# Attention and spectral mixing on one core: last rows of two batches by narrow products, fill products in PE's last waits, last tiles sent by two engines

## The chip, the cores and the metric

The kernel runs on one core of one Trainium2 chip. A time is the device time of one execution in microseconds (us). Comparisons are between medians of several runs. TensorE is called PE, VectorE DVE, ScalarE ACT, GpSimd POOL and SyncE SP, as in the profile.

## The reference

First a sliding-window attention with 8 batches, 8 heads, 576 positions and head size 64, window 64. Its output is x, 8 x 576 x 512. Then a spectral mix along the sequence: the 64 lowest Fourier modes of x are multiplied by one complex 512 x 512 matrix for each mode, and transformed back. Last a projection with a ReLU.

```python
scores = np.where((rel >= 0) & (rel < 64), q @ k.T / np.sqrt(D), -1e9)
x = softmax(scores) @ v                       # to (B, S, 512)
X = np.fft.rfft(x, axis=1)[:, :64]
Y = einsum('bmd,mde->bme', X, w_r + 1j * w_i) # 64 matrices for each of w_r, w_i
y = np.fft.irfft(Y, n=S, axis=1)
u = x + y
out = u + np.maximum(u @ w_ch, 0.0)           # float32, 8 x 576 x 512
```

The two stacks of 64 matrices are 134 MB in float32.

## The kernel before, in words

The order of the work is written out by hand, engine by engine; tile pools add the waits. POOL's DMA queue brings the weights and casts them to bf16 on the way, two modes (or, near the end, one) in a transfer, into two rings of buffers and into space that is lent.

*Attention* runs first, beside the first weight loads. It leaves x in `x_sb` and `x4` and its forward transform in `XQ`.

*The spectral half.* Modes go in 16 groups of four. `steps` lists the groups by halves of the channels (`hb`), and each step has a part with w_r and a part with w_i (`ri`). `mode_half` (line 162) makes one such part: 8 products (line 171) whose weights are 32 columns of `XQ` and whose moving operand is a weight tile; the four modes of a group fill four row blocks of one PSUM bank `psm`. Groups 12 and 13 (`LAST` and `LAST + 1`) come last. In the very last part the order is by mode, and the last two modes have a transfer each, so that PE can start on each as it lands. `finish_group` (line 595) casts a finished group to bf16 (`stg`); the inner function `prepare` puts it in order by products with `sel`: transposed into `pt` (line 612), and for groups 12 and 13 also as rows into `py` (line 619).

Between the parts PE has other products to do, which `advance` deals out: `transposed` and `multiply` give XW = x @ w_ch for each of the 36 output tiles (`x_jobs`), and `batch_job` gives for each batch the rows Y (`yrows`) and Z = Y @ w_ch (`zrows`). Y and Z have 128 rows of modes for each batch. Batch 0 has tiles of its own, `Y0` and `Z0`; the others lie in `Yall` and `Zall`. The 16 rows that come from groups 12 and 13 are not there yet at that point and are put in later.

*The inverse transform and the output.* 36 tiles of 128 positions: for each batch four, and after each pair of batches one with the last 64 positions of both. A tile i needs

- u = x + trigI^T Y: `tail_x` (an identity product that puts x into PSUM bank `pu[i]`), `tail_u` (products with `trigI`, then a copy to SBUF by ACT; for odd tiles below 33 there is no identity product, and DVE adds x instead: `by_dve`);
- p = XW + trigIr^T Z: `tail_xw` (an identity product) and the product with `trigIr` in `tail_out`;
- out = u + relu(p): in `tail_out`, by DVE at line 756, or, for the tiles of `by_dve`, by ACT and POOL at line 754. SP sends the tile to memory (line 760); a tile with the last positions of two batches goes in two halves.

`tail_u` runs four tiles ahead (`AHEAD`).

*Around the change.* After the last wi product PE makes `tail_xw(0)` and `tail_xw(1)`, and then the two groups' last rows are finished for all batches together: `prepare` for group 13 (here called `select`), a copy of `pt` to `tr` by ACT, a copy of `py` to `yst` by DVE, four products `pz` = tr^T w_ch (line 774), a copy to `zst` (line 780). Two DMAs by SP spread `yst` and `zst` over the rows of `Yall` and `Zall` (lines 770 and 781). Batch 0, with which the output begins, does not wait for them: products with every eighth column of an identity (lines 777 and 785) pick its 16 rows out of `yst` and `zst`, and copies put them into `Y0` and `Z0` (lines 778 and 786).

```python
        y0 = bank("y")
        nc.tensor.matmul(out=y0[0:16], lhsT=ident_bf[:, 0:128:B], rhs=yst, start=True, stop=True)
        z0 = bank("p")
        nc.tensor.matmul(out=z0[0:16], lhsT=ident_r[:, 0:128:B], rhs=zst, start=True, stop=True)
```

Of the kernel before, what the change touches and what calls it, by code (L numbers as in the profile page):

```python
# [11 lines left out]
BF16 = mybir.dt.bfloat16  # L12
# [14 lines left out]
def kernel(  # L27
# [41 lines left out]
    sel = consts.tile([128, 4, 16], BF16, name="sel")  # L69
    trigF = consts.tile([128, NTF, 2 * NM], BF16, name="trigF")  # L70
# [93 lines left out]
    def mode_half(psm, grp, hb, ri, first, last):  # L164
        pairs = range(4 * grp, 4 * grp + 4)
        order = [(j, p) for j in range(NJ) for p in pairs]
        if (grp, hb, ri) == (*steps[-1], 1):
            order.sort(key=lambda jp: (jp[1], jp[0]))
        for j, p in order:
            g = p % 4  # L170
            nc.tensor.matmul(out=psm[32 * g:32 * g + 32, :],  # L171
# [6 lines left out]
        spent.update(i for i, (_, ps, *of) in enumerate(wlist) if ps[0] in pairs and of == [hb, ri])  # L178

    with tc.manual_schedule():  # L180
# [321 lines left out]
        stgpool = pool("stgpool", bufs=4, reuse_waits="tile")  # L502
        Y0 = zpool.tile([128, DM], BF16, name="Y0")
        Z0 = zpool.tile([128, DM], FP32R, name="Z0")
        rowpool = pool("rowpool", reuse_waits="tile")
# [57 lines left out]
        def yrows(b):  # L563
            return Yall[:, b, :] if b else Y0

        def zrows(b):
            return Zall[:, b, :] if b else Z0
# [27 lines left out]
        def finish_group(grp, psm):  # L595
# [12 lines left out]
            rows = slice(16 * (grp // 2), 16 * (grp // 2) + 16)  # L608

            def prepare():  # L610
# [3 lines left out]
                if not end:  # L614
                    if i:
                        k0 = 8 * (grp - 1)
                        nc.scalar.copy(out=YT[:, :, :, k0:k0 + 16], in_=pt.rearrange("p c (k b) -> p b c k", b=B))
                    return
                nc.tensor.matmul(out=py[64 * i:64 * i + 64, :], lhsT=lanes, rhs=stg, start=True, stop=True,
                                 tile_position=(0, 64 * i))  # L620
            if grp == LAST + 1:
                late["last"] = prepare, rows
            else:
                ready.append(prepare)
# [32 lines left out]

        stmp2 = pool("stmp2", side="right", reuse_waits="tile")
        tables = list(inverse_tables())
        NX0 = 10  # L660
        x_jobs(pool("xp0", reuse_waits="tile"), 0, NX0)
        psm = None
        half = given = 0
        n0, n1 = 2 * EARLY, 4 * (NGRP - EARLY)
        for i, (grp, hb) in enumerate(steps[EARLY:]):
            f, l = grp < EARLY or hb == 0, hb == 1
            if i == EARLY:
                while tables:
                    tables.pop(0)()
                while jobs or pend:  # L670
                    advance()
                close(stmp2, yp, ringB)
                Zall = pool("zall", side="right").tile([2 * NM, B, DM], FP32R, name="Zall")
                x_jobs(pool("xp1", side="right", reuse_waits="tile"), NX0, NT)
                given = 0
            if f:
                psm = bank("m")
            for ri in range(2):
                if half == n0 + n1 - 2:
                    while jobs or pend:  # L680
                        advance()
                mode_half(psm, grp, hb, ri, f, l)
                load_weights(len(wlist))
                while ready:
                    ready.pop(0)()
                for t in tables[0:2]:
                    t()
                del tables[0:2]
                if half == 0:
# [100 lines left out]
        for i in range(NT):  # L790
            tail_out(i)
            if i > 1:
                tail_xw(i + 2)
# [35 lines left out]
```

## Time and profile before

| | |
|---|---|
| median of 3 runs | 442.08 us (441.78 to 442.22) |
| profiled execution | 441.96 us |
| its span | 440.2 us |
| PE busy | 330.7 us (75%) |
| DVE busy | 219.8 us (50%) |
| ACT busy | 172.8 us (39%) |
| POOL busy | 143.3 us (33%) |
| mean granted PE clock | 0.897 |

The span is from the first to the last instruction of the core; some 1.8 us of the execution lie outside it. Times in rows of the trace count from the start of the span. Matmuls overlap, and their ends are modelled, so a busy PE is not PE at its peak. In rows of the timeline stand start, duration, engine (PEld is the loading of PE's weights), line, operation, out<-in, shapes, count, and in brackets the idle time ahead with what ended it. In rows of groups, busy time and the mean ns of one follow the first bar, idle time ahead the second. In windows, PEclk is the granted clock as a share of full speed, and the DMA share is the mean of 16 DMA engines.

### The profile page before, as it was taken

How to read it: one execution, taken by the hardware profiler on the slowest of the kernel's cores; microseconds unless marked ns; L12 is line 12 of the kernel's file. 1: busy time of each engine (PE TensorE's matmuls, PEld its weight loads, DVE VectorE, ACT ScalarE, POOL GpSimd, SP SyncE). 2: the span in 40 equal slices, each digit the busy share in tenths (PEclk: the TensorE clock that was granted, in tenths of full speed). 3: DMA queues.
4: the chain of work that ended last, by engine and by line, in shares of the span. 5: the costliest groups of instructions: out<-in, count | busy, mean ns of one | idle time of the engine just before them, and what ended most of it. 6: DMA issues, size and time to landing. Idle time of an engine off the chain costs nothing.

```text
span 440.2 us, 10911 instructions
## 1 busy us (share of the span) xinstructions
PE 330.7 (75%) x4670; PEld 211.8 (48%) x4712; DVE 219.8 (50%) x445; ACT 172.8 (39%) x304; POOL 143.3 (33%) x211
## 2 busy tenths in 40 slices
PE   6888989898999997974335564675766676669994
PEld 3666767676667675651113222333443443334552
DVE  8488777876776774865004111212223122335773
ACT  6566757565666664532001110111221122113662
POOL 9333333323333223222232322122322223200773
PEclk8699999999999998997559666789899889997999
DMA  8999999999999999999999999999999999982787
GB/s 206 211 211 211 212 211 210 211 211 211 211 212 211 211 211 212 210 211 211 214 255 211 211 211 211 211 211 211 211 211 211 211 211 211 212 167 60 268 296 274
DMA packets 47873, 93.45 MB, mean 212 GB/s; under 512 B 3536, under 2 KB 3664, under 8 KB 47824
## 3 DMA queue, kind: packets, MB, share of 16 engines
q0 software_dynamic: 42000, 81.73, 98.4%
q1 hardware_dynamic: 5824, 11.01, 7.3%
q8 instruction: 37, 0.61, 0.5%
q14 instruction: 12, 0.10, 0.1%
HBM read 163.58 MB, written 9.44 MB: 393 GB/s over the span
## 4 chain that ended last, share of the span: by engine, by line
DMA 42%; PE 40%; issue 8%; DVE 3%; ACT 3%; POOL 1%; DVEq 0%; POOLq 0%
DMA wr<-in_moe_w_r_dram 35%; PE tr L214 6%; PE s L261 5%; PE s L273 4%; PE pt L281 4%; PE vb L226 4%; DMA rawk<-in_k_dram 4%; DMA wi<-in_moe_w_i_dram 3%; PE psm L171 3%; PE o L301 3%; PE s L253 2%; PE psm L720 1%; PE px L324 1%; PE pst L746 1%; PE psz L720 1%
## 5 line engine op out<-in xcount | busy, mean ns | idle before, releaser
L155 POOL DMA_DIRECT2D wi<-in_moe_w_i_dram x62 | 44.0, 710 | 92.8 <-PE psm L171 36.5
L171 PEld LDWEIGHTS <-XQ 128*32 128x32 bf16 x512 | 24.1, 165 | 96.3 <-issue 89.0
L655 DVE CAST xw<-psz 128x512 fp32r<-128x512 f32 x36 | 24.9, 691 | 90.6 <-PE psz L579 90.6
L579 PE MATMUL psz<-wch,tr 128*128 128x512 f32 x176 | 61.4, 480 | 11.0 <-DMA wch<-in_moe_w_ch_dram 11.0
L155 POOL DMA_DIRECT2D wr<-in_moe_w_r_dram x53 | 37.9, 715 | 84.2 <-PE psm L171 44.0
L171 PE MATMUL psm<-wi,XQ 128*32 128x512 bf16 x244 | 34.2, 453 | 39.9 <-DMA wi<-in_moe_w_i_dram 39.9
L265 DVE TENSOR_REDUCE mx<-s 128x4 fp32r<-128x512 f32 x72 | 49.5, 688 | 27.9 <-PE s L261 27.6
L556 ACT CAST tr<-ptx 128x512 fp32r<-128x512 bf16 x36 | 21.1, 587 | 106.1 <-PE ptx L572 106.1
L171 PE MATMUL psm<-wr,XQ 128*32 128x512 bf16 x212 | 27.9, 448 | 27.3 <-DMA wr<-in_moe_w_r_dram 26.7
L275 ACT ACTIVATE p<-s 128x512 bf16<-128x512 f32 x72 | 39.8, 604 | 13.6 <-PE s L273 13.6
L579 PEld LDWEIGHTS psz<-wch,tr 128*128 128x128 f32 x176 | 35.9, 226 | 16.8 <-issue 11.2
L261 PE MATMUL s<-kT,qT 64*64 64x128 bf16 (+1 forms) x576 | 29.4, 223 | 6.9 <-issue 6.9
L218 ACT COPY kT<-tr 128x576 bf16<-128x576 bf16 x32 | 23.2, 724 | 23.4 <-PE tr L214 23.3
L754 POOL TENSOR_TENSOR ut<-ut,XQ 128x512 f32<-128x512 f32 x16 | 20.5, 1284 | 29.2 <-DVE ut L738 23.0
L284 DVE COPY pts<-pt 128x1024 bf16<-128x1024 bf16 (+1 forms) x40 | 25.2, 629 | 6.6 <-PE pt L281 5.2
L218 ACT COPY qT<-tr 128x576 bf16<-128x576 bf16 x32 | 23.3, 728 | 9.8 <-PE tr L214 9.5
L273 PE MATMUL s<-mx,ident_r 128*128 128x512 f32 x72 | 26.9, 446 | 0.0
L261 PEld LDWEIGHTS <-qT 64*64 64x64 bf16 x576 | 18.0, 108 | 18.4 <-issue 17.9
L218 ACT COPY vT<-tr 128x576 bf16<-128x576 bf16 x32 | 23.3, 728 | 4.2 <-PE tr L214 4.1
L281 PE MATMUL pt<-ident_bf,p 128*128 128x128 bf16 x288 | 23.8, 223 | 1.5 <-issue 1.3
L598 DVE TENSOR_TENSOR stg<-psm,Ypair 128x512 bf16<-128x512 f32 x10 | 6.9, 690 | 35.1 <-PE psm L171 35.1
L313 DVE TENSOR_TENSOR x_sb<-o,r 128x512 bf16<-128x512 f32 x32 | 22.1, 691 | 1.1
(172 smaller groups left out, 559.5 us busy)
## 6 DMA issues: line engine op xcount, KB each, us to landing
wi<-in_moe_w_i_dram POOLq DMA_DIRECT2D x60, 512.0 KB, 15.9
wr<-in_moe_w_r_dram POOLq DMA_DIRECT2D x53, 512.0 KB, 16.4
out_dram<-ut SPq DMA_DIRECT2D x32, 256.0 KB, 2.3
rawv<-in_v_dram POOLq DMA_DIRECT2D x16, 288.0 KB, 14.6
rawk<-in_k_dram POOLq DMA_DIRECT2D x15, 288.0 KB, 13.4
rawq<-in_q_dram POOLq DMA_DIRECT2D x15, 288.0 KB, 13.7
Ypair<-in_moe_w_r_dram POOLq DMA_DIRECT2D x5, 512.0 KB, 14.9
x_sb<-in_moe_w_r_dram POOLq DMA_DIRECT2D x4, 512.0 KB, 15.3
```

The source lines that it names most:

```text
L155: nc.gpsimd.dma_start(out=w[:, 0:len(ps)], in_=src[ps[0]:ps[-1] + 1, HALF * hb:HALF * hb + HALF, :].rearrange("g (p j) e -> p g j e", j=NJ))
L171: nc.tensor.matmul(out=psm[32 * g:32 * g + 32, :], lhsT=XQ[hb].rearrange("k s b m -> k (s b) m")[:, (3 * j + 1 - ri) * B:(3 * j + 5 - ri) ...
L214: nc.tensor.transpose(out=pt[ro, j, :], in_=raw[ro, TH * half + j, :], identity=ident_bf[ro, ro])
L218: nc.scalar.copy(out=to, in_=pt.rearrange("p j n -> p n j"))
L261: nc.tensor.matmul(out=s[ro, t, lo:128], lhsT=lq, rhs=kT[ro, 64 * n - 64 + lo:64 * n + 64], start=False, stop=True, skip_group_check=True)
L265: nc.vector.tensor_reduce(out=mx, in_=s, axis=AX.X, op=ALU.max, negate=True)
L273: nc.tensor.matmul(out=s, lhsT=ident_r, rhs=mx.unsqueeze(2).to_broadcast([128, 4, 128]), start=False, stop=True, skip_group_check=True)
L275: nc.scalar.activation(out=p[:, 4 * c2:4 * c2 + 4, :], in_=s, func=ACT_F.Exp, scale=EX_SCALE)
L281: nc.tensor.transpose(out=pt[:, t, :], in_=st[u]["p"][:, t, :], identity=ident_bf)
L284: nc.vector.tensor_copy(out=ps[:, 0:nt, :], in_=pt[:, 0:nt, :])
L579: nc.tensor.matmul(out=pz, lhsT=tr[:, c, :], rhs=wch[:, c, :], start=(c == 0), stop=(c == NDCH - 1))
L655: nc.vector.tensor_copy(out=XW[i], in_=pz)
```

## The change

Three things are changed.

1. *Rows of batches 0 and 1.* Both batches now have tiles of their own (`Y0`, `Z0`, `Y1`, `Z1`). Their last 16 rows of Y come from `stg` itself: `put_first` multiplies it with `pick`, a selection matrix with 16 columns for each batch, once for group 12 and once for group 13, into rows 0 to 15 and 32 to 47 of one bank. Their rows of Z: batch 0's come from four products of w_ch with every eighth column of `tr`; batch 1's are picked out of `zst`, as batch 0's were before. `tr` is now filled in two halves, one for each group (`take`), and lies in `Zall`'s space for batch 0, which is free. The products for all batches (`put_y`, `pz`) and the DMAs to `Yall` and `Zall` come after those for batch 0, interleaved with the first output tiles.
2. *Products in PE's waits.* Ahead of the last part of the spectral half stand five products whose result nobody uses (`keep_warm`), the part of `put_first` for group 12, and `tail_xw(0)`, `tail_xw(1)`, `tail_x(0)`. Two unused products stand ahead of each of the last two modes.
3. *Last tiles.* Of the last four tiles, ACT's queue sends tile 33 and the first half of tile 35; SP sends the others.

To make room `stgpool` has two buffers instead of four. Functions of the output (`tail_x` and so on) move up in the file unchanged, but for the engine that sends. The core of the diff:

```diff
+        ending = (grp, hb, ri) == (*steps[-1], 1)
...
+            if ending and j == 0 and g >= 2:
+                keep_warm(2)
...
+    def keep_warm(n):
+        for _ in range(n):
+            nc.tensor.matmul(out=late["warm"], lhsT=ident_bf, rhs=late["zeros"], start=True, stop=True)
...
+            yield lambda: ve.memset(pick, 0.0)
+            yield lambda: ve.tensor_copy(out=pick[:, :, 8:16], in_=sel.rearrange("p g (r b) -> p b (g r)", b=B)[:, 0:2])
...
-        stgpool = pool("stgpool", bufs=4, reuse_waits="tile")
+        stgpool = pool("stgpool", bufs=2, reuse_waits="tile")
...
+            def put_first():
+                for b in range(2):
+                    nc.tensor.matmul(out=late["first"][32 * b:32 * b + 16, :], lhsT=pick[:, b, 8 - 8 * i:24 - 8 * i],
+                                     rhs=stg, start=(i == 0), stop=(i == 1), tile_position=(0, 32 * b))
+            def take():
+                nc.scalar.copy(out=late["tr"][:, :, 64 * i:64 * i + 64], in_=pt[:, :, 64 * i:64 * i + 64])
...
-                nc.sync.dma_start(out=o, in_=ut[n * h:n * h + n, :])
+                by = nc.scalar if i >= NT - AHEAD and (i + h) % 2 else nc.sync
+                by.dma_start(out=o, in_=ut[n * h:n * h + n, :])
...
+                if half == n0 + n1 - 1:
+                    late["warm"], late["zeros"] = bank("z"), trigI[:, 0:DM]
+                    keep_warm(5)
+                    late["first"] = bank("z")
+                    late[0][1]()
+                    tail_xw(0)
+                    tail_xw(1)
+                    tail_x(0)
                 mode_half(psm, grp, hb, ri, f, l)
...
+        turn()
+        take()
+        put_first()
+        nc.vector.tensor_copy(out=Y0[rows], in_=first[0:16])
+        nc.scalar.copy(out=Y1[rows], in_=first[32:48])
+        z0 = bank("z")
+        for c in range(NDCH):
+            nc.tensor.matmul(out=z0[0:16], lhsT=tr[:, c, 0:128:B], rhs=wch[:, c, :],
+                             start=(c == 0), stop=(c == NDCH - 1))
+        tail_u(0)
+        put_y()
+        nc.vector.tensor_copy(out=Z0[rows], in_=z0[0:16])
         yst = rowpool.tile([128, DM], BF16, name="yst")
-        nc.vector.tensor_copy(out=yst, in_=late["py"])
+        nc.scalar.copy(out=yst, in_=late["py"])
         nc.sync.dma_start(out=Yall[rows], in_=yst)
+        tail_u(1)
+        pz = bank("p")
         for c in range(NDCH):
             nc.tensor.matmul(out=pz, lhsT=tr[:, c, :], rhs=wch[:, c, :], start=(c == 0), stop=(c == NDCH - 1))
+            if c == 0:
+                tail_out(0)
+        zst = trpool.tile([128, NDCH, 128], FP32R, name="tr").rearrange("p c k -> p (c k)")
         nc.vector.tensor_copy(out=zst, in_=pz)
         nc.sync.dma_start(out=Zall.bitcast(FP32)[rows], in_=zst.bitcast(FP32))
+        tail_u(2)
         tail_xw(2)
+        tail_out(1)
+        z1 = bank("p")
+        nc.tensor.matmul(out=z1[0:16], lhsT=ident_r[:, 1:128:B], rhs=zst, start=True, stop=True)
+        nc.scalar.copy(out=Z1[rows], in_=z1[0:16])
+        tail_u(3)
+        tail_u(4)
         tail_xw(3)
+        tail_u(5)
+        for i in range(2, NT):
             tail_out(i)
+            tail_xw(i + 2)
             tail_u(i + AHEAD)
```

The lines that made `y0` and `z0` out of `yst` and `zst`, and `tail_xw(0)`, `tail_xw(1)`, `tail_x(0)` behind the last part, go. DVE's and ACT's other work is unchanged.

More of the change, by code (lines that the diff above doesn't have):

```diff
@@ new lines @@
+        rows = slice(8 * LAST, 8 * LAST + 16)
+        turn, put_first, take, put_y = late[1]
+        tr, first = late["tr"], late["first"]
+        turn()
+        take()
+        put_first()
[5 more added lines that the diff above has]
+                             start=(c == 0), stop=(c == NDCH - 1))
@@ L778 @@
-        nc.scalar.copy(out=Y0[rows], in_=y0[0:16])
-        zst = rowpool.tile([128, DM], FP32R, name="zst")
+            if c == 0:
+                tail_out(0)
+        zst = trpool.tile([128, NDCH, 128], FP32R, name="tr").rearrange("p c k -> p (c k)")
         nc.vector.tensor_copy(out=zst, in_=pz)
         nc.sync.dma_start(out=Zall.bitcast(FP32)[rows], in_=zst.bitcast(FP32))
+        tail_u(2)
         tail_xw(2)
-        tail_u(0)
-        z0 = bank("p")
-        nc.tensor.matmul(out=z0[0:16], lhsT=ident_r[:, 0:128:B], rhs=zst, start=True, stop=True)
```

143 lines of the change are left out of this document (65 added, 78 removed).

## The prediction

> **What bounds the kernel now.** The page comes first, for the whole span.
>
> ```profile
> span 440.2 us, 10911 instructions
> PEclk8699999999999998997559666789899889997999
> DMA  8999999999999999999999999999999999982787
> DMA 42%; PE 40%; issue 8%; DVE 3%; ACT 3%; POOL 1%; DVEq 0%; POOLq 0%
> ```
>
> A slice is 11 us. The DMA engines are full for 35 slices: they bring the weights, and DMA is the longest part of the chain. The change leaves what is loaded, and in which order, as it was. So I take the last weights to land at the same time, and only what follows can move. The timeline of that stretch, lines left out:
>
> ```profile
> 382.55 0.29 PE L612 MATMUL psp<-sel,stg 128*128 128x64 bf16 x4
> 383.54 0.58 ACT L634 COPY Yall<-ptx 128x512 bf16<-128x512 bf16 x1 [4.18 <-PE ptx L633]
> ...
> 391.90 0.68 PE L171 MATMUL psm<-wr,XQ 128*32 128x512 bf16 x6 [0.33 <-DMA wr<-in_moe_w_r_dram]
> 394.34 1.09 PE L171 MATMUL psm<-wi,XQ 128*32 128x512 bf16 x4 [1.76 <-DMA wi<-in_moe_w_i_dram]
> 395.86 1.01 PE L171 MATMUL psm<-wi,XQ 128*32 128x512 bf16 x2 [0.43 <-DMA wi<-in_moe_w_i_dram]
> 397.07 1.01 PE L171 MATMUL psm<-wi,XQ 128*32 128x512 bf16 x2 [0.20 <-DMA wi<-in_moe_w_i_dram]
> 398.01 1.22 PE L746 MATMUL pst<-xw,ident_r 128*128 128x512 f32 x2
> 398.12 0.69 DVE L600 CAST stg<-psm 128x512 bf16<-128x512 f32 x1 [6.19 <-PE psm L171]
> 399.03 0.44 PE L612 MATMUL psp<-sel,stg 128*128 128x64 bf16 x4
> 399.56 0.58 ACT L556 CAST tr<-psp 128x512 fp32r<-128x512 f32 x1 [8.95 <-PE psp L612]
> 400.20 1.32 PE L774 MATMUL psz<-wch,tr 128*128 128x512 f32 x3
> 401.79 0.49 PE L774 MATMUL psz<-wch,tr 128*128 128x512 f32 x1
> 402.32 0.69 DVE L780 CAST zst<-psz 128x512 fp32r<-128x512 f32 x1 [1.56 <-PE psz L774]
> 403.07 0.42 PE L785 MATMUL psp<-zst,ident_r 128*16 128x512 f32 x1
> 403.52 0.68 DVE L786 CAST Z<-psp 16x512 fp32r<-16x512 f32 x1 [0.51 <-PE psp L785]
> 404.26 0.50 PE L720 MATMUL pst<-Z,trigIr 128*128 128x512 f32 x1
> ```
>
> The last weights let PE start at 397.07. The last product of the spectral half ends at 398.08. From there a single thread runs to 404.26: cast, transposition, copy, four products with w_ch, cast, selection, copy, first product of tile 0's output. That is 6.2 us in which PE does only 20 products. The windows give the clock in it, and what bounds the rest:
>
> ```profile
> core 0: us, PE busy (x) PEld busy (x) DVE busy (x) ACT busy (x) POOL busy (x), PEclk, DMA share, GB/s
> 370.28:373.69 3.41, 1.68 (x14) 1.09 (x13) 0.43 (x2) 0.58 (x1) 0.89 (x2) 1.00 1.12 210
> 387.34:390.76 3.42, 3.42 (x23) 2.40 (x20) 1.65 (x3) 1.17 (x2) 0.00 (x0) 1.00 1.12 210
> 390.76:394.17 3.41, 1.49 (x10) 0.39 (x9) 0.76 (x2) 0.00 (x0) 0.00 (x0) 1.00 0.74 141
> 394.17:397.58 3.41, 2.61 (x8) 0.49 (x7) 0.00 (x0) 0.00 (x0) 0.00 (x0) 0.50 0.31 56
> 397.58:401.00 3.42, 3.42 (x12) 1.72 (x11) 1.38 (x2) 0.58 (x1) 0.00 (x0) 0.50 0.00 0
> 401.00:404.41 3.41, 3.17 (x12) 1.25 (x11) 1.55 (x3) 1.38 (x3) 0.00 (x0) 1.00 0.17 47
> 407.00:433.00 26.00, 26.00 (x113) 14.68 (x114) 18.28 (x29) 17.33 (x32) 19.72 (x16) 1.00 0.84 290
> ```
>
> From 394.17 to 401.00 PE runs at half clock. The window before that had 1.49 us of PE work in 3.41; the clock fell at its end. 1.68 us, in the window from 370.28, was enough to hold it. A window of 2.61 us did not bring it back, a full one did. After 407 PE is busy for all of 26.00 us and no other engine is, so the output stage is bound by PE, at 26.00/113 = 0.230 us a product.
>
> The Trainium skill, TensorE: Matmul & The Clock Gate, Part 1, has the same two clocks and a free window of 3413 ns, but gives "≥1 idle window" as the cause of the fall. This trace differs: the window before the fall was 44% busy.
>
> **The change, part by part.** Two stretches are to be priced: up to the first output product, and from it to the end.
>
> *Fill.* In the last half step PE is idle from 392.58 to 394.34. There it now gets five unused products, the two of `put_first` for group 12, `tail_xw(0)`, `tail_xw(1)` and `tail_x(0)`. They start at about 392.6 at full clock, ten times 0.23 us, so until 394.9. The wi products of 394.34 are queued behind them and start some 0.6 us late. That costs nothing as long as PE is back for the last pair: four wi products at full clock take at most 4 x 0.23 = 0.9 us (395.8), two unused ones 0.46 (396.3), the pair of 395.86 0.46 (396.7), two more unused 0.46 (397.2). So PE is ready at 397.0 to 397.2, against 397.07. The last pair, 1.01 us at half clock, becomes 0.5 to 0.6: end at 397.7 instead of 398.08. Every 3.41 us from 392.6 on now holds over 1.68 us of PE work, so I take the clock as full to the end.
>
> *First rows without the detour.* From 397.7, durations from the rows above and these:
>
> ```profile
> L329 ACT CAST XQ<-px 128x256 bf16<-128x256 f32 x16 | 6.0, 372 | 11.8 <-PE px L326 11.6
> L720 PE MATMUL pst<-Z,trigIr 128*128 128x512 f32 x2 | 1.1, 540 | 0.0
> ```
>
> Cast to `stg` 0.04 + 0.69: 398.45. `turn`, 0.29 at full clock (the row of 382.55), no longer behind `tail_xw`: 398.8. `take` copies half the columns, 0.37: 399.2. Meanwhile PE does the two `put_first` products and DVE copies rows of Y0 (0.68, 399.45 to 400.1). z0, four products with 16 columns of weights, now straight from `tr`: 4 x 0.23 + 0.15 from 399.25, so 400.35. The width of the weights does not shorten a product (the 16-column one of 403.07 took 0.42). Copy to Z0 0.68: 401.1. The first output product stands behind `tail_u(0)`, `put_y`, `tail_u(1)` and one pz product, done by 401.2. It starts at 401.1 to 401.3 instead of 404.26: **3.0 us** earlier.
>
> *What is late next.* PE's output stage. The code gives its products: before, 147 follow the last wi product, 20 of them ahead of tile 0's output, 127 from it on. Now 149 follow, 14 ahead, 135 from it on: three pz products, `tail_x(2)`, the product of `tail_u(2)`, `tail_xw(2)`, `tail_xw(3)` and z1 come later than they did. Eight times 0.23 = 1.85 us are given back. One wait is added: z1 needs `zst`, and DVE casts that only after Z0, tile 1's sum and tile 0's output (0.68 + 0.69 + 0.68 + 0.69 from 400.4, so 403.15), while PE reaches z1 after eight products at 403.0. That is 0.2 us, and what is queued behind it is tile 3's product. ACT's Y1 waits for DVE's Y0, Z1 for z1 (about 404.3); tile 4's row of Z1 is wanted some 2 us later. The transfers of yst and zst move past tile 0's output on SP; they feed tiles 8 and later, over 4 us on. So PE ends its last product 3.0 - 1.85 - 0.2 = **about 1.0 us** earlier. Without the clock the two orders are about even: half clock costs the old thread some 1.2 us (the last pair 0.45, `tail_xw` and `turn` ahead of the first copy 0.3, the products at 400 some 0.45), and nearly all of the gain is that.
>
> *The end.* Rows of the timeline, then the last output transfers by their line, then windows:
>
> ```profile
> 432.30 1.29 POOL L754 TENSOR_TENSOR ut<-ut,XQ 128x512 f32<-128x512 f32 x1 [0.55 <-ACT XQ L753]
> 432.51 1.29 DVE L756 SCALAR_TENSOR_TENSOR ut<-psz,ut 128x512 f32<-128x512 f32 x2 [1.33 <-PE psz L720]
> 434.31 0.68 DVE L756 SCALAR_TENSOR_TENSOR ut<-pst,ut 128x512 f32<-128x512 f32 x1
> ...
> L760 SPq DMA_DIRECT2D out_dram<-ut x8: 332/372/594, 431.8 to 436.4; - x8
> DMA to landing us min/median/max: 2.0/2.5/2.9
> 434.00:435.00 1.00, 0.00 (x0) 0.00 (x0) 0.99 (x2) 0.00 (x0) 0.00 (x0) 1.00 0.63 231
> 435.00:436.00 1.00, 0.00 (x0) 0.00 (x0) 0.00 (x0) 0.00 (x0) 0.00 (x0) 1.00 1.02 379
> 436.00:437.00 1.00, 0.00 (x0) 0.00 (x0) 0.00 (x0) 0.00 (x0) 0.00 (x0) 1.00 1.03 379
> ```
>
> The last DVE sum ends at 434.99, but SP starts its last issue only at 436.4: eight issues stand in one queue, and tile 31, which POOL ends at 433.59, holds up tile 32. Tile 33 and half of tile 35 now go by ACT. If the queue were all, 1.4 us would be won. But the DMA engines are full at 379 GB/s from 435 to 437: 0.76 MB, three of the last tiles, pass there as fast as they can, so most of it is bandwidth. And a wait is added: the last issue, the second half of tile 35 on SP, shares its semaphore with tile 33's transfer on ACT, and waits for that to land. Tile 33's sum, the second of the two from 432.51, ends at 433.8 - 1.0; its transfer takes 2.0 to 2.9 us; the last half then 2.0 to 2.6. That lands it at 432.8 + 4.0 to 432.8 + 5.5, so 436.8 to 438.3, against 436.4 + 2.6 - 1.0 = 438.0 had only PE moved. I take 0.3 us won, nearer to the late end since three tiles share the engines then; bounds 1.0 won (bandwidth allows no more) and 0.3 lost. No transfer by ACT is in this trace; an extra microsecond for its first one is my outer bound.
>
> The Trainium skill, DMA: Bandwidth & Descriptors, says transfers issued by several engines run on the same 16 DMA engines and only issue time is saved. The rows of 435 to 437 agree; by that rule the split would win nothing while those rows are full.
>
> *Small things.* `pick` costs DVE two short operations early on, under the weight loads. `stgpool` with two buffers still leaves a group its buffer until the next but one. `take` for group 12 adds 0.37 us to ACT at 383, where the row of 383.54 shows 4.18 us of idle time. Nothing.
>
> **Sum.** The profiled execution took 441.96 us (span 440.2). 441.96 - 1.0 - 0.3 = 440.7. The median of the runs shown is 442.08, 0.1 more, so I forecast **440.8 us**.
>
> **Rivals.** *The clock is already down when the fill starts* (it ends slower). The fill and the products pulled ahead then run at 0.43 us, as the wi pairs of 395.86 did: ten before wi (4.3 us, to 396.9), then 12 more of wi and fill (up to 5.2): the last pair ends 2 to 3 us later than 398.08, while the thread after it wins back about 1. Some 1.5 to 2.4 us slower, 444.0. It decides if a 3.41 us window that ends shortly ahead of 392.6 has less than about 1.5 us of PE work. Against it: the window from 387.34 is full (3.42 of 3.42), and the clock is 1.00 up to 394.17. 8 in 100.
>
> *The end gives back what PE wins.* Tile 33's landing is late because three tiles share the engines, or ACT's first transfer is slow, and the last half leaves PE's 1.0 us earlier but lands no earlier. Time: 441.7 to 442.5, 442.1 taken. For it: the added wait is in the program, and the end hangs on transfers, not on PE. 20 in 100. The same time comes out if the fill fails to hold the clock between 398 and 401, where PE still has short waits: the first-row thread would lose about 1 us there.
>
> *The end wins more.* Tile 33 lands in 2.0 us and the two queues keep the engines full: 1.2 from PE and 0.8 to 1.0 at the end, 440.0. 15 in 100.
>
> **How the numbers follow.** Forecast case 57, slower rival 8, even rival 20, better end 15. The forecast's own bounds are 440.2 (0.3 more at PE, 0.3 more at the end) and 441.4. A measurement of this kernel tells 0.2% from no change, 0.9 us. Below 441.2 lie the better end and about nine tenths of the forecast case: 0.66. The even rival and the rest of the forecast are within 0.9 us, less a little that goes beyond 443: 0.24. Slower 0.10. The range leaves out the slower rival and a few hundredths at the low end: 439.9 to 442.5.
>
> **What would show it.** Right: granted clock 1.00 through 394 to 401; last wi product ended by 397.8; tile 0's output product on PE 3.4 to 3.6 us after that; PE's last product about 1 us earlier; SP's last issue waiting for a landing. Wrong: a 0.50 in the window rows after 394; wi products that start behind the landing of their weights for the last pair; a wait of over 0.5 us at z1; the last transfer landing over 5.5 us after PE's last product.

## Result: 0.25% faster

The changed kernel took 441.3 us (median of 12 runs, 441.01 to 442.19), the kernel before 442.35 (median of 12, 441.78 to 443.29): a ratio of 0.9975, 95% interval 0.9966 to 0.9984. The forecast was 440.8, range 439.9 to 442.5, "faster" with a chance of 0.66.

The profiled execution took 441.02 us. Its page, the lines that answer to the first ones of the prediction:

```profile
span 439.2 us, 10995 instructions
PEclk9999999999999996988559556788889689899999
```

The slices from 384 us on are all 9 now; before, the one from 396 had a 7. The changed kernel's timeline, where the half step ends, where the output stage begins, and at the end (start, duration, engine, line, operation; lines left out):

```profile
396.79 0.61 PE L186 MATMUL psz<-trigI,ident_bf 128*128 128x512 bf16 x2
397.33 0.65 PE L175 MATMUL psm<-wi,XQ 128*32 128x512 bf16 x2
398.01 0.69 DVE L612 CAST stg<-psm 128x512 bf16<-128x512 f32 x1 [5.65 <-PE psm L175]
398.76 0.29 PE L623 MATMUL psp<-sel,stg 128*128 128x64 bf16 x4 [0.79 <-DVE stg L612]
399.08 0.37 ACT L636 CAST Zall<-psp 128x256 fp32r<-128x256 f32 x1 [8.03 <-PE psp L623]
399.51 1.11 PE L808 MATMUL psz<-wch,Zall 128*16 128x512 f32 x4
400.65 0.68 DVE L812 CAST Z<-psz 16x512 fp32r<-16x512 f32 x1
401.67 0.39 PE L697 MATMUL pst<-Z,trigIr 128*128 128x512 f32 x1
...
402.84 0.68 DVE L823 CAST tr<-psp 128x512 fp32r<-128x512 f32 x1
403.27 0.40 PE L697 MATMUL pst<-Z,trigIr 128*128 128x512 f32 x1
403.58 0.42 PE L829 MATMUL psp<-tr,ident_r 128*16 128x512 f32 x1
...
431.36 1.30 POOL L731 TENSOR_TENSOR ut<-ut,XQ 128x512 f32<-128x512 f32 x1 [0.54 <-ACT XQ L730]
432.24 0.63 PE L697 MATMUL pst<-Zall,trigIr 128*128 128x512 f32 x2
433.37 0.68 DVE L733 SCALAR_TENSOR_TENSOR ut<-pst,ut 128x512 f32<-128x512 f32 x1
```

The last wi pair (L175) follows its two unused products (L186) with no pause and runs at full clock. It ends at 397.98, 0.1 earlier than before. The thread from there to tile 0's first output product (L697 with Z) now ends at 401.67 instead of 404.26. The cast of `zst` (L823) ends at 403.52 and z1 (L829) starts at 403.58. Windows of the changed kernel, with the columns of the prediction's windows: four clock windows, the output stage, and four slices of 1 us at the end.

```profile
389.50:392.92 3.42, 3.34 (x19) 1.67 (x18) 2.26 (x4) 0.58 (x1) 0.00 (x0) 1.00 0.93 174
392.92:396.33 3.41, 3.41 (x17) 1.21 (x16) 0.00 (x0) 0.00 (x0) 0.00 (x0) 1.00 0.52 97
396.33:399.74 3.41, 2.48 (x13) 0.77 (x14) 0.69 (x1) 0.37 (x1) 0.00 (x0) 1.00 0.03 5
399.74:403.16 3.42, 3.42 (x15) 1.80 (x14) 2.89 (x5) 1.65 (x3) 0.00 (x0) 1.00 0.01 2
407.00:433.00 26.00, 25.87 (x113) 14.58 (x112) 18.64 (x30) 16.43 (x31) 19.27 (x15) 1.00 0.87 299
433.00:434.00 1.00, 0.00 (x0) 0.00 (x0) 1.00 (x2) 0.00 (x0) 0.00 (x0) 1.00 0.64 231
434.00:435.00 1.00, 0.00 (x0) 0.00 (x0) 0.05 (x1) 0.00 (x0) 0.00 (x0) 1.00 1.04 381
435.00:436.00 1.00, 0.00 (x0) 0.00 (x0) 0.00 (x0) 0.00 (x0) 0.00 (x0) 1.00 1.03 381
436.00:437.00 1.00, 0.00 (x0) 0.00 (x0) 0.00 (x0) 0.00 (x0) 0.00 (x0) 1.00 0.97 264
```

The granted clock is 1.00 in all rows. PE is as full in the output stage as before, and the end looks as before too: a hole in the transfers from 433 to 434, then full engines. The output sends, grouped by their line (duration in ns minimum/median/maximum, first and last start):

```profile
L738 SPq DMA_DIRECT2D out_dram<-ut x7: 332/398/472, 429.7 to 435.5; - x7
L738 ACTq DMA_DIRECT2D out_dram<-ut x2: 382/458/533, 432.9 to 434.1; - x2
DMA to landing us min/median/max: 2.0/2.6/3.9
```

ACT issues at 432.9 and 434.1. SP's last issue starts at 435.5, when ACT's first transfer has landed (435.41 by the trace).

The table gives the key times of every profiled execution, read from the traces. The landing of the last weights differs by up to 0.9 us from one to the next, so the other times are counted from it, in us. The times of PE's last product are its start. The two columns on the right are of all timed runs; a ratio is to the kernel before as timed beside that run (its medians lie between 442.24 and 442.66), so where runs are compared, the ratios count for more than the medians.

| kernel | last weights land | last wi product ends | first output product | PE's last product starts | last output lands | median (lowest to highest) | ratio to before, interval |
|---|---|---|---|---|---|---|---|
| before | 397.02 | +1.06 | +7.24 | +36.39 | +41.99 | 442.35 (441.78–443.29) | – |
| changed | 397.21 | +0.76 | +4.46 | +35.27 | +40.87 | 441.3 (441.01–442.19) | 0.9975 (0.9966–0.9984) |
| fill_alone | 397.48 | +0.63 | +6.13 | +35.34 | +40.97 | 441.39 (441.12–442.16) | 0.9978 (0.9966–0.9989) |
| rows_alone | 397.51 | +1.04 | +4.96 | +35.80 | +41.41 | 441.87 (441.38–442.67) | 0.9984 (0.9974–0.9994) |
| no_unused | 397.20 | +0.64 | +5.70 | +36.50 | +42.46 | 442.72 (441.01–443.45) | 1.0 (0.9985–1.0016) |
| no_split | 397.89 | +0.94 | +4.63 | +35.43 | +41.04 | 441.34 (441.04–442.18) | 0.9975 (0.9965–0.9986) |
| unused_only | 397.20 | +0.93 | +6.46 | +35.61 | +41.21 | 441.31 (440.97–441.57) | 0.9976 (0.9964–0.9988) |
| free_split | 397.08 | +0.87 | +4.57 | +35.38 | +41.04 | 440.92 (440.69–441.14) | 0.9963 (0.9949–0.9977) |
| long_fill | 397.11 | +2.43 | +6.13 | +36.94 | +42.59 | 443.01 (442.37–443.74) | 1.001 (1.0–1.0021) |
| more_dve | 396.95 | +0.90 | +4.61 | +34.60 | +40.92 | 441.53 (441.0–442.11) | 0.9979 (0.997–0.9988) |
| dve4 | 397.16 | +0.94 | +4.64 | +34.64 | +40.35 | 440.67 (440.34–440.87) | 0.996 (0.9948–0.9972) |
| dve4_31 | 397.29 | +0.89 | +4.59 | +34.59 | +39.94 | 440.52 (440.08–441.68) | 0.9961 (0.9946–0.9976) |
| dve8_31 | 397.37 | +0.93 | +4.63 | +33.82 | +39.89 | 439.89 (439.7–440.19) | 0.9944 (0.9932–0.9957) |
| dve8_31_oldrows | 397.06 | +0.63 | +6.15 | +33.77 | +39.09 | 439.68 (439.23–440.11) | 0.9936 (0.9922–0.9949) |

The changed kernel starts its output stage 2.78 us earlier by this measure, but PE ends only 1.12 earlier, and the last output lands the same 1.12 earlier.

### The profile page after: what moved, and what is told of

It is laid out like the page before. It is cut to its first block, busy times and chain, and to the rows that moved or that the text cites. A ratio compares the mean times of both kernels' runs of the same rounds, so it can differ in the third digit from the quotient of the medians.

```text
span 439.2 us, 10995 instructions
## 1 busy us (share of the span) xinstructions
PE 350.0 (80%) x4728; PEld 219.5 (50%) x4728; DVE 219.9 (50%) x447; ACT 173.7 (40%) x307; POOL 143.4 (33%) x211
## 4 chain that ended last, share of the span: by engine, by line
DMA 47%; PE 41%; issue 5%; ACT 3%; DVE 3%; POOL 1%; DVEq 0%; POOLq 0%
DMA wi<-in_moe_w_i_dram 24%; DMA wr<-in_moe_w_r_dram 11%; DMA rawk<-in_k_dram 7%; PE tr L222 6%; DMA wch<-in_moe_w_ch_dram 4%; PE s L269 4%; PE pt L289 4%; PE s L261 4%; PE s L281 3%; PE psm L175 3%; PE vb L234 3%; PE o L309 2%; PE psz L591 1%; PE psm L697 1%; PE pst L723 1%
## 5 line engine op out<-in xcount | busy, mean ns | idle before, releaser
L591 PE MATMUL psz<-wch,tr 128*128 128x512 f32 x176 | 67.2, 517 | 10.9 <-DMA wch<-in_moe_w_ch_dram 10.9
L175 PEld LDWEIGHTS <-XQ 128*32 128x32 bf16 x512 | 24.0, 165 | 81.0 <-issue 73.6
L175 PE MATMUL psm<-wi,XQ 128*32 128x512 bf16 x244 | 34.0, 466 | 30.6 <-DMA wi<-in_moe_w_i_dram 30.6
L591 PEld LDWEIGHTS psz<-wch,tr 128*128 128x128 f32 x176 | 40.1, 252 | 17.4 <-issue 11.2
L175 PE MATMUL psm<-wr,XQ 128*32 128x512 bf16 x212 | 29.8, 485 | 22.0 <-DMA wr<-in_moe_w_r_dram 21.3
L261 PE MATMUL s<-mask_t,ident_bf 128*128 128x512 bf16 x72 | 28.4, 395 | 0.9 <-ACT p L283 0.8
```

The source lines that it names most:

```text
L175: nc.tensor.matmul(out=psm[32 * g:32 * g + 32, :], lhsT=XQ[hb].rearrange("k s b m -> k (s b) m")[:, (3 * j + 1 - ri) * B:(3 * j + 5 - ri) ...
L261: nc.tensor.matmul(out=s, lhsT=ident_bf, rhs=mask_t[:, mk], start=True, stop=True)
L591: nc.tensor.matmul(out=pz, lhsT=tr[:, c, :], rhs=wch[:, c, :], start=(c == 0), stop=(c == NDCH - 1))
```

## Experiments

The theory behind the prediction: the gain is the clock that the fill holds, while the narrow rows mostly move eight products from ahead of the first output to behind it. Rivals: the shorter thread of the rows pays by itself; or the two sending queues pay.

### Which part pays: one part alone, or all but one

**fill_alone**: the kernel before with the fill. Without narrow rows there is no `put_first` to pull ahead, so three useful products go ahead here and nine unused ones.

```
 # ahead of the last half step                   # in mode_half, last half step
+late["warm"], late["zeros"] = bank("z"), ...    +if ending and j == 0 and g >= 2:
+keep_warm(5)                                    +    keep_warm(2)
+tail_xw(0); tail_xw(1); tail_x(0)
 # after finish_group: the same three
-tail_xw(0); tail_xw(1); ...; tail_x(0)
```

> The kernel before with the fill alone: five unused products, tile 0's and 1's XW products and tile 0's x product ahead of the last wi part, two unused ones ahead of each of its last two modes. Rows and output queue as before. Theory 1 (the gain is the clock): granted clock 1.00 from 394 to 404, the first output product on PE about 6.2 - 1.4 = 4.8 us behind the last wi product instead of 6.2, the last PE product 1.2 to 1.4 us earlier than before, 441.0 us against 442.35. Rival (the gain is the shorter thread for the first rows): within 0.4 us of before, since half a microsecond of PE at half clock is hidden under the casts and copies.

**rows_alone**: the changed kernel without the fill, the useful products pulled ahead put back behind the half step, and all sends by SP.

```
-keep_warm(5); late[0][1](); tail_xw(0); tail_xw(1); tail_x(0)    # ahead of the last half step
-    keep_warm(2)                                                 # inside it, twice
+tail_xw(0); tail_xw(1)                                          # after it, ahead of turn() and take()
+late[0][1]()                                                    # behind them
+nc.sync.dma_start(out=o, ...)
```

> The narrow products for the rows of batches 0 and 1 alone: no unused products, tile 0's and 1's XW products and the first rows' products of group 12 behind the last wi part, all tiles sent by SP. Theory 1: the clock falls to 0.50 at 394 as before, the first output product comes 1 to 1.5 us earlier, but eight more products follow it (1.85 us), so the last PE product is 0 to 0.5 us later than before, 442.3 to 442.9 us. Rival: the shorter thread carries the gain, 441.3 us with the clock at 0.50.

**no_unused**: the changed kernel without its nine unused products. The five useful ones stay ahead.

```
-keep_warm(5)        # ahead of the last half step
-    keep_warm(2)    # inside it, twice
```

> The changed kernel without its nine unused products; the useful ones stay pulled ahead of the last wi part. If the unused products are needed to hold the clock: 0.50 in some window from 394 to 402, the last PE product 0.5 to 1.3 us later than in the changed kernel, 441.8 to 442.6 us. If the five useful ones suffice: clock 1.00, PE free when the last weights land, the last wi product 0.1 to 0.3 us nearer to the landing than in the changed kernel (0.77 us behind it there), 441.0 to 441.3 us. By the windows' threshold (between 1.49 and 1.68 us of work in 3.41) it hangs on where the window lies, so a spread between runs is possible.

**no_split**: the changed kernel, all outputs sent by SP.

```
-by = nc.scalar if i >= NT - AHEAD and (i + h) % 2 else nc.sync
-by.dma_start(out=o, ...)
+nc.sync.dma_start(out=o, ...)
```

> The changed kernel with all output sent by SP. In the changed kernel the last transfer landed 5.6 us behind the start of PE's last product, against 5.4 before. Theory (the semaphore wait behind ACT's transfer gives back what the second queue wins): 5.4 us again, the time within 0.2 us of the changed kernel, 441.1 to 441.3 us. Rival (the second queue is worth something): 0.3 us or more slower than the changed kernel, 441.6 us.

Measured: fill_alone has the ratio of the whole change, 0.9978, and lands its last output 1.02 us earlier, counted from the landing, where the changed kernel does so 1.12 us earlier. The clock is 1.00 throughout, and the rival is out. The theory's sizes were too large: from the last wi product to the first output product it took 5.50 us, not 4.8, PE's last product came 1.05 earlier, not 1.2 to 1.4, and the median is 441.39, not 441.0. The 1.4 us were counted from the end of the wi products, but 0.43 of the gain lie ahead of it (+0.63 against +1.06).

no_split is the changed kernel to the last digit of the ratio: the second queue is worth nothing that the times resolve. It lands 5.61 us after PE's last product; the 5.4 us that its expectation gives for the kernel before are 5.60 by the trace.

no_unused falls back to 1.0, with a wide spread: two of its twelve executions took 441.01 and 441.03, the other ten 442.17 to 443.45. The five useful products do not hold the clock reliably; that it held in those two would fit, but the one execution profiled is one of the ten. Its clock windows, the last with weights to wait for and the one after:

```profile
395.88:399.29 3.41, 1.79 (x10) 0.54 (x9) 0.69 (x1) 0.34 (x1) 0.00 (x0) 1.00 0.06 11
399.29:402.70 3.41, 3.32 (x8) 1.09 (x9) 1.37 (x2) 1.55 (x4) 0.00 (x0) 0.50 0.01 2
```

The first row's PE work is 1.79 of 3.41 us, and the clock is 0.50 in the next. There the narrow rows' thread runs at half clock, and its first output product comes 1.24 us later than in the changed kernel (5.70 against 4.46). The windows of rows_alone:

```profile
391.57:394.98 3.41, 1.37 (x10) 0.39 (x9) 0.69 (x1) 0.00 (x0) 0.00 (x0) 1.00 0.63 120
394.98:398.39 3.41, 2.93 (x8) 0.48 (x7) 0.00 (x0) 0.00 (x0) 0.00 (x0) 0.50 0.23 42
398.39:401.81 3.42, 3.29 (x18) 1.15 (x17) 1.87 (x3) 0.78 (x2) 0.00 (x0) 1.00 0.01 2
```

Here the clock is down for one window where the profile of before had two: after a window with 2.93 us of work it came back, after one of 2.61 us it had not. rows_alone gains 0.16%, small, but its interval (0.9974 to 0.9994) leaves out 1, where the prediction had the two orders "about even" without the clock. Neither theory's numbers came: the first output product is 2.28 us earlier, not 1 to 1.5, PE's last product 0.59 earlier, not later, and 441.87 lies below the first theory's 442.3 and above the rival's 441.3. Whether the shorter thread or the luck of the windows gave it, one profile of each does not tell.

### Are the unused products alone enough?

**unused_only**: fill_alone without the three useful products pulled ahead.

```
 keep_warm(5)
-tail_xw(0); tail_xw(1); tail_x(0)                  # ahead of the last half step
+tail_xw(0); tail_xw(1); ...; tail_x(0)             # after it, as in the kernel before
```

> The kernel before with the nine unused products alone: five ahead of the last half step, two and two inside it. No useful product is pulled ahead, and rows, order and sends are those of before. Theory that the clock is what pays: granted clock 1.00 from 394 to 401, the first output product some 0.8 to 1.2 us earlier than in the kernel before, and a time 0.6 to 1.0 us below it; the run with useful and unused products together was 0.8 us below. Theory that the useful products pulled into the idle time are what pays: less than 0.3 us below the kernel before. If nine products are too few for the clock, a row of 0.50 after 394 and a time as before.

Measured: 0.9976, the changed kernel's ratio. The windows of unused_only, in which products that compute nothing stand in PE's waits:

```profile
390.52:393.94 3.42, 3.37 (x18) 1.45 (x17) 1.50 (x3) 0.59 (x1) 0.00 (x0) 1.00 0.73 137
393.94:397.35 3.41, 2.30 (x11) 0.83 (x10) 0.00 (x0) 0.00 (x0) 0.00 (x0) 1.00 0.39 72
397.35:400.76 3.41, 3.21 (x14) 1.34 (x13) 1.38 (x2) 0.58 (x1) 0.00 (x0) 1.00 0.00 0
400.76:404.17 3.41, 3.23 (x12) 1.31 (x12) 1.91 (x3) 1.75 (x3) 0.00 (x0) 1.00 0.28 67
```

The clock stays at 1.00 and the first output product comes at +6.46, 0.8 earlier than before: the first theory's numbers. So nine unused products, with rows, order and sends as they were, give a time that cannot be told from that of the whole change. What the rest adds in the profiles, +41.21 to +40.87, is below what the times resolve.

### Does the end hang on PE's thread?

**long_fill**: seven more unused products in front of the wi products.

```
-keep_warm(5)
+keep_warm(12)
```

> The changed kernel with twelve unused products instead of five ahead of the last half step, 7 x 0.23 = 1.6 us more in front of the wi products. In the changed kernel PE was through with its fill 0.12 us after the last weights had landed, so no slack is left: theory, the last wi product ends 1.6 us later than there, at about 399.6, and the kernel is 1.5 us slower than the changed one, 442.8, slower than the one before. Rival, that PE's start of the output stage hangs on other engines and not on this thread: less than 0.8 us slower.

Measured: last wi product 1.67 us later from the landing (2.43 against 0.76), first output product 1.67 later, last output 1.72 later, and a median of 443.01, 1.7 above the changed kernel's. The theory's numbers, to 0.2 us: there is no slack anywhere between the fill and the end. It also shows the price of a fill that is too long: 1.6 us of it turn the gain into a time that is no better than before.

### What the end is made of

**free_split**: both halves of the last tile by ACT, all else by SP, so no send waits for a landing of the other queue.

```
-by = nc.scalar if i >= NT - AHEAD and (i + h) % 2 else nc.sync
+by = nc.scalar if i == NT - 1 else nc.sync
```

> The changed kernel, with the sends of the last four tiles dealt out otherwise: both halves of the last tile by ACT, tiles 32 to 34 by SP, so that no issue has to wait until a transfer of the other queue has landed. In the changed kernel SP's last issue waited so from 434.10 to 435.43. Theory that this wait cancelled a gain of the second queue: from PE's last product to the last landing 5.0 to 5.3 us instead of 5.60, and a time 0.3 to 0.6 us below the changed kernel's. Theory that the last transfers are bound by the DMA engines, which ran full at 379 GB/s at the end: 5.5 to 5.7 us, and the same time within 0.2 us.

Measured: the last issue starts at 434.64 instead of 435.51, and the last output lands 5.66 us after PE's last product instead of 5.60. That is the second theory's number. The median is 0.4 us below the changed kernel's, which is the first theory's; but the two intervals overlap for most of their width, so a gain in time is neither shown nor excluded. End slices of free_split:

```profile
434.00:435.00 1.00, 0.00 (x0) 0.00 (x0) 0.03 (x1) 0.00 (x0) 0.00 (x0) 1.00 1.04 383
435.00:436.00 1.00, 0.00 (x0) 0.00 (x0) 0.00 (x0) 0.00 (x0) 0.00 (x0) 1.00 1.06 305
436.00:437.00 1.00, 0.00 (x0) 0.00 (x0) 0.00 (x0) 0.00 (x0) 0.00 (x0) 1.00 0.93 240
437.00:438.00 1.00, 0.00 (x0) 0.00 (x0) 0.00 (x0) 0.00 (x0) 0.00 (x0) 0.52 0.57 207
```

And of no_split, where one queue sends all (its landing lies 0.8 us later):

```profile
435.00:436.00 1.00, 0.00 (x0) 0.00 (x0) 0.00 (x0) 0.00 (x0) 0.00 (x0) 0.84 1.02 375
436.00:437.00 1.00, 0.00 (x0) 0.00 (x0) 0.00 (x0) 0.00 (x0) 0.00 (x0) 0.50 1.03 383
437.00:438.00 1.00, 0.00 (x0) 0.00 (x0) 0.00 (x0) 0.00 (x0) 0.00 (x0) 0.50 1.00 277
```

In both the engines are full (shares near 1) until the last microsecond. In free_split the last transfers are issued sooner, but they do not pass sooner: the rate falls to 305 and 240 GB/s while the share stays at 1.06 and 0.93.

**more_dve**: free_split's sends, and four even tiles treated as the odd ones are.

```
-    return i % 2 == 1 and i < NT - 3
+    return (i % 2 == 1 or i in (6, 12, 18, 24)) and i < NT - 3
-rt = spare[i // 2 % len(spare)]
+rt = spare[late.setdefault("rt", 0) % len(spare)]
+late["rt"] += 1
```

> The changed kernel with the sends as in the run of both last halves by ACT, and with tiles 6, 12, 18 and 24 treated as the odd tiles are: DVE adds x, ACT does the relu, POOL the last sum, and PE has four identity products fewer. Theory that the output stage is bound by PE at 0.23 us a product: PE ends 4 x 0.23 = 0.9 us earlier, 0.8 to 1.0 us faster than the run with the sends alone. Rival: POOL, at 1.29 us a tile and 19.7 us of 26 us busy in that stage, then holds up the sends or the buffers, and nothing or less than 0.3 us is won.

Measured: PE's last product 0.78 earlier than in free_split (34.60 against 35.38), but the last output only 0.12 earlier, and a median of 441.53, above free_split's 440.92. Nothing is won, as the rival says. Two windows of more_dve, and then a row of its timeline:

```profile
407.00:420.00 13.00, 12.95 (x56) 7.34 (x56) 9.53 (x16) 9.08 (x17) 12.20 (x11) 1.00 0.81 284
420.00:433.00 13.00, 11.95 (x52) 6.77 (x51) 9.24 (x15) 7.86 (x15) 11.20 (x9) 1.00 0.93 314
```

```profile
424.89 5.01 POOL L732 TENSOR_TENSOR ut<-ut,XQ 128x512 f32<-128x512 f32 x4
```

POOL (the fifth busy column) is at 12.20 of 13 us, and from 424.89 it does four tiles without a pause. The sends show what that costs: by the trace those of tiles 24 to 28 start 29.3 to 32.8 us after the landing of the last weights, no sooner than in free_split and up to 0.2 us later, although PE ends 0.78 ahead. dve4, below, which leaves these tiles to DVE, sends them 0.7 to 0.8 earlier than free_split. So POOL held up the sends there. The last send starts 0.6 us earlier than in free_split, but by then the transfers stand behind one another on full engines (shares of 1.02 to 1.06 from 432 to 436).

**dve4**: the same four tiles by DVE alone, which leaves POOL as it was. **dve4_31**: tile 31 in the list too. **dve8_31**: eight even tiles and tile 31.

```
+def alone(i):
+    return i in (6, 12, 18, 24)                            # dve4
+    return i in (6, 12, 18, 24, 31)                        # dve4_31
+    return i in (4, 8, 12, 14, 18, 22, 26, 28, 31)         # dve8_31
 def by_dve(i):
-    return i % 2 == 1 and i < NT - 3
+    return alone(i) or i % 2 == 1 and i < NT - 3
 ...
-if by_dve(i):                       # in tail_out: ACT's relu and POOL's sum
+if by_dve(i) and not alone(i):
```

> The changed kernel, sends of the last four tiles as in the run with both last halves by ACT, and tiles 6, 12, 18 and 24 finished by DVE alone: DVE adds x where PE's identity product and ACT's copy did, and does the relu and sum as before. POOL's share stays. PE has four products fewer (0.92 us). Theory that the output stage is bound by PE and that the run with these tiles on POOL lost its 0.9 us to POOL (12.2 of 13 us busy): 0.7 to 0.9 us below the run with the sends alone, whose median was 440.92, so about 440.1. Rival, that the transfers of the outputs bound the end whatever PE does: less than 0.3 us won, 440.7 or more.

> The kernel of the four tiles by DVE alone, with tile 31 by DVE alone too. In the changed kernel POOL ended tile 31 at 432.65 and its send, 432.68, stood ahead of those of tiles 32 to 34 in SP's queue, while the DMA engines were 0.64 busy from 433 to 434. Theory that this hole is part of the end: another 0.3 to 0.4 us won. Rival, that DVE, which has no pause in its last three sums, gets late by 0.69 us: nothing won or up to 0.4 us lost against the run without tile 31.

> The same with eight even tiles (4, 8, 12, 14, 18, 22, 26, 28) and tile 31 by DVE alone: eight products fewer on PE, 1.8 us, and DVE gets some 5.5 us more in a stage in which it is busy 18.6 of 26 us. Theory that PE stays the bound: a further 0.6 to 0.9 us below the run with four tiles and tile 31. Rival, that the DMA engines, 0.92 busy from 420 to 433 in the changed kernel, or DVE take over: 0.3 us or less.

Measured for dve4: 0.74 us at PE (34.64 against 35.38), much as in more_dve, and now 0.69 of it reach the last landing. The median fell by only 0.25 us against free_split's, to 440.67, within both intervals: the theory's mechanism shows in the profile, but in the time the number is the rival's, and the theory's 0.7 to 0.9 us are not there. For tile 31, one row of dve4 and then one of dve4_31:

```profile
432.00:433.00 1.00, 0.20 (x1) 0.00 (x0) 1.00 (x3) 0.00 (x0) 0.00 (x0) 1.00 0.65 242
```

```profile
432.00:433.00 1.00, 0.27 (x2) 0.00 (x0) 1.00 (x3) 0.00 (x0) 0.00 (x0) 1.00 1.05 389
```

The hole, 0.65 busy, is filled, and the last output lands 0.41 earlier in the profile, as the theory had it; the medians, 0.15 apart, do not confirm it. dve8_31: 0.77 earlier at PE than dve4_31, 0.05 at the last landing, and 0.63 at the median (439.89, ratio 0.9944, an interval that lies wholly below the changed kernel's). The time says the theory, the single profile says the rival. The profiled execution, at 440.17, is one of the two slowest of its five, so the median is the better evidence; but the intervals of dve4_31 and dve8_31 overlap (0.9946 to 0.9976 and 0.9932 to 0.9957), so this step is likely and not shown. What is shown is the gain over the changed kernel, of tiles and sends together: no run has these tiles with the changed kernel's sends, and free_split's sends may hold up to 0.4 us of it.

**dve8_31_oldrows**: the same, with the old first rows and fill_alone's fill (three useful products ahead, not five as the expectation has it).

```
 # on fill_alone:
+by_dve, alone and tail_out as in dve8_31
-nc.sync.dma_start(out=o, ...)
+by = nc.scalar if i == NT - 1 else nc.sync
+by.dma_start(out=o, ...)
```

> The kernel before with all of the fill (five useful products pulled ahead, nine unused), with tiles 4, 8, 12, 14, 18, 22, 26, 28 and 31 by DVE alone and both last halves sent by ACT, but with the old first rows: the detour over yst and zst, and no 16-column products. It asks whether the narrow rows are worth anything once DVE takes some of PE's work. Theory that they only move products about, 2.0 us won ahead of the first output product and eight products given back behind it: within 0.3 us of the run with the narrow rows, whose median was 439.89 at a ratio of 0.9944. Theory that the earlier start of the transfers counts now that the DMA engines are full for the last 7 us: 0.5 us or more slower than that run.

Measured: 439.68, ratio 0.9936, the fastest of all, within 0.3 us of dve8_31: the first theory. Its first output product comes 1.52 us later from the landing than in dve8_31, and PE still ends 0.05 earlier, because 127 products follow instead of 135, less what DVE took. Four rows of its windows:

```profile
407.00:420.00 13.00, 13.00 (x58) 7.42 (x56) 12.80 (x22) 6.25 (x11) 10.60 (x9) 1.00 0.91 321
420.00:433.00 13.00, 11.22 (x49) 6.38 (x47) 10.98 (x18) 6.11 (x11) 7.32 (x6) 1.00 0.94 326
...
432.00:433.00 1.00, 0.00 (x0) 0.00 (x0) 0.41 (x1) 0.00 (x0) 0.00 (x0) 1.00 1.04 377
433.00:434.00 1.00, 0.00 (x0) 0.00 (x0) 0.00 (x0) 0.00 (x0) 0.00 (x0) 1.00 1.02 383
```

The second theory, 0.5 us or more slower, is out. The output stage is now near three limits at once: PE 13.00 and DVE 12.80 of 13 us, and the DMA engines at a share of 0.91 to 1.04.

## Why the prediction was right, point by point

*Fill.* Right in the mechanism: clock 1.00 throughout, and this is the gain (fill_alone, unused_only; no_unused loses it). The price of half clock was right too: some 1.2 us were forecast for the old thread, 0.45 of them at the last pair; fill_alone's first output product comes 1.11 us earlier, 0.43 at the last pair. What the clock needs was read less well. That 1.68 us of work in a window had held it is no safe mark, since 1.79 did not hold it in no_unused. It did no harm because the emptiest window of the changed kernel in this stretch has 2.48. The time of the last pair was off by a quarter microsecond: the last pair ended at 397.98, not 397.7. The weights landed 0.19 later than before, and the fill was through 0.12 after that (the row of 397.33), where the prediction had PE ready just in time. The place where it says that being late "costs nothing" had no margin left, and long_fill puts the price of lateness at one for one. That the last pair starts behind its landing was one of the prediction's own signs of being wrong; it came, by 0.12 us.

*First rows without the detour.* 2.6 us earlier instead of 3.0. Of the 0.4 missing, 0.27 are the late pair; from its end to tile 0's product it took 3.7 us against 3.4 to 3.6. The steps between stand in the timeline as forecast (0.69, 0.29, 0.37, 1.11, 0.68 us); but the copy to Z0 ends at 401.33, and PE starts the product only at 401.67. The products queued ahead of it were to be done by 401.2, and the last of them, the first of the pz products, only starts at 401.25.

*What is late next.* Right: eight products more follow tile 0's output, and they take back most of it. The stretch from tile 0's first output product to PE's last grew from 29.15 to 30.81 us, so 1.66 were given back against 1.85 + 0.2. The wait at z1 was less than 0.1 us (the cast ends at 403.52, the product ahead of z1 started at 403.27, z1 at 403.58), since Z0, tile 1's sum and tile 0's output kept DVE no longer than PE's queue. That the term came out so close is in part luck: 0.4 us less were won ahead of the first output product and 0.4 less given back behind it. PE ended 0.9 us earlier by the clock of the span, 1.12 from the landing, where 1.0 was forecast.

*"Without the clock the two orders are about even."* Confirmed where the clock is the same in both: with the clock held, unused_only and dve8_31_oldrows are as fast as their partners with the narrow rows. rows_alone gained 0.16% where the sentence gives nothing; that is open.

*The end.* This term was mis-sized: 0.3 us won were forecast, 0.00 measured (5.60 us from PE's last product to the last landing, before and after), and no_split loses nothing by going back. The added wait came as described: SP's last issue waits for tile 33's landing on ACT's queue (435.41) and starts at 435.51, 1.5 us after DVE's last sum. But the wait was not what ate the gain: free_split has no such wait, and in its profile lands no sooner. The engines are full at the end in both: from 435 to 437 before (shares 1.02 and 1.03), from 434 to 437 after (1.04, 1.03 and 0.97). "Over 5.5 us" from PE's last product to the last landing was another sign of being wrong; it came, but could tell nothing, as the kernel before has 5.60 too. The Trainium skill, DMA: Bandwidth & Descriptors, "Issuing engines are not separate DMA queues", has it that transfers started by several engines share the same 16 DMA engines and that only issue time is saved; the 5.60, 5.61 and 5.66 us of the changed kernel, no_split and free_split agree.

*Sum.* 1.3 us were forecast, 1.05 measured at the medians: 1.0 of PE's term and nothing of the end's 0.3. The even rival's "end gives back" did not happen, and neither did the better end. The slower rival did not arise; its own sum does not close, since 396.9 + 5.2 = 402.1 is 4 us behind 398.08, where it says 2 to 3.

## What to carry to other kernels

Look for the wait in which the clock falls before redesigning the thread behind it: nine products that compute nothing, put where PE waits for its last weights, did what the whole change did, but the fill must end when the weights land, as each microsecond beyond that is lost. A thread cut short gains only as much as it does not hand on: count the products that come later instead. In a stage bound by one engine, take work off that engine and give it to one with room: POOL, nearly full, gained nothing (more_dve), and with nine tiles by DVE alone and other sends the time fell further than by the whole change (dve8_31). Here the last transfers filled the DMA engines, and a second issuing queue by itself did not land them sooner after PE's last product (5.60 and 5.66 us in two profiles, against 5.60 and 5.61 with one).

## Not expected of the hardware

The number of products in a clock window does not tell whether the clock falls; their busy time does, but for a narrow band. Of the windows quoted that ran at full clock, those with 10 products (1.37, 1.49 and 1.79 us) were followed by half clock, those with 11 or more by full clock. Other windows of the same traces break that rule: in unused_only one with 16 products and 1.75 us of work (from 359.80) was followed by half clock, in dve8_31_oldrows one with 9 products and 1.98 us (from 429.24) by full clock. Over all windows of the 14 traces, some 1350 at full clock, half clock followed each with less than 1.62 us of work in its 3.41 us, full clock each with more than 1.91; of the 61 between, 23 were followed by half clock. Whether that band is the chip's or comes from the modelled ends of the products stays open. The Trainium skill, TensorE: Matmul & The Clock Gate, Part 1, names at least one idle window as the cause; a window that is 52% busy (1.79 of 3.41 us) was enough here.

At the end the DMA engines moved less at the same share: 305 and 240 GB/s at 1.06 and 0.93 in free_split, 264 at 0.97 in the changed kernel, both with two queues. One queue does it too, later: 375 and 383 GB/s at 1.02 and 1.03 in no_split, then 277 at 1.00. Which transfers slow one another down was not tried.
